# The gradient of an output projection, moved from the attention stage of a fused backward kernel to its last stage

## The chip, the core and the metric

The kernel runs on one NeuronCore of a Trainium2 chip. The core has a matrix engine (TensorE, PE in the profile; its weight loads are shown as PEld), three engines for elementwise work (VectorE or DVE, ScalarE or ACT, GpSimd or POOL), a queue engine (SyncE or SP) that issues most transfers, and 16 DMA engines that carry them. Matrix products land in PSUM, eight banks of 2 KB per partition, and are copied ("evacuated") from there to SBUF by VectorE or ScalarE. The metric is the device time of one execution in microseconds.

## The reference

A gated mix of a sliding-window attention A and a gated feed-forward block B, and the gradients of all its inputs but B_x, which is not used:

```python
q, k, v = qkv[0], qkv[1], qkv[2]                 # 32 heads of 16, from x @ wqkv
scores = jnp.einsum("bhqd,bhkd->bhqk", q, k) * (Dh ** -0.5)
mask = (idx[:, None] - idx[None, :] >= 0) & (idx[:, None] - idx[None, :] < W)   # W = 256
p = _softmax(jnp.where(mask[None, None], scores, -1e9), axis=-1)
o = jnp.einsum("bhqk,bhkd->bhqd", p, v)
a = o.reshape(B, S, D) @ wo
...
h = relu(x @ W_gate) * (x @ W_up);  b = h @ W_down
g = _sigmoid((x * gate_w).sum(-1, keepdims=True))
out = g * a + (1 - g) * b
_grads = _vjp(grad_out)
```

B = 1, S = 2048, D = 512, F = 1376, all in bfloat16. With da = g * grad_out, the gradient of wo (dWo, `out_3`, 512 x 512) is the product of o transposed and da, summed over the 2048 rows.

## The kernel before

Rows are cut into 16 tiles of 128 (t, or q and k for query and key blocks), D into four slices of 128 (c; each holds 8 heads), F into 11 chunks. Three stages follow each other.

**Feed-forward stage.** For every chunk of F and every 512 rows PE makes the gate, the up product and dh; the results h, dgate and dup go transposed to DRAM (`hgu_d`) and PE sums the gradients of W_gate, W_up and W_down. In the same turns `make_da` (L314) scales grad_out by g, and `turn_da` (L319) stores a tile of da in DRAM (`da_d`) and transposes it into SBUF (`da_T`).

**Attention stage.** The loop at L970 runs turns: per slice c 46 of them, each with two pairs of heads. A turn makes scores S and D (L714), the exponential (ScalarE, L747), the mask (GpSimd, L757), the product PP (VectorE, L764), transposes of it by PE (L818) or by DMA (L810), row sums BA (L781, L783) and the products CD (L495, L498) that give dk and dv. `small_ops` (L821) writes dq and o, CD's evacuation dk and dv, into `sts[c]`, 16 tiles by four columns of 128: index 0 to 2 are dq, dk, dv, index 3 is o. It is spilled to `dqkvo_d` in DRAM (L506). PE's remaining time in a turn is filled from a list `bg` of priced pieces: the projections of the next 512 rows (`project_parts`, L137), in c = 0 the rest of the feed-forward gradients (`tail_parts`), and in c = 1, 2, 3 the weight gradients of slice c - 1 (`grad_parts`, L567): first part DC, which is dWo (16 matmuls of 512 columns, L606, with the rows of da loaded back from `da_d`), then four parts of dWqkv (64 matmuls of 384 columns, L603). L990 says how many parts begin in each quarter of a slice: (0, 1, 2, 2). A list `late` holds the loads and transposes of weights for the last stage, popped every second turn (L1070).

**The seam.** After the last turn SP loads what the last stage needs for its first two tiles: `early_group` (L860) the transposed dq, dk, dv and o, `load_group(0)` (L898) the rest, among it duT_g; then the last transposes of W_up into SBUF (L1082), whose last chunk is padded by a GpSimd memset (`clear`, L528), which waits for the transposes. The gradients of slice c = 3 are done here, as `S2["grads"]`: dWqkv for the first 12 tiles within the last turns, then dWo, then dWqkv for the last four tiles. Their stores go over GpSimd's queue (L590).

**Last stage.** Eight groups of two tiles (L1107). For a tile PE makes b in `bps` (11 matmuls of 512 columns, L1117), a in `aps` (4, L1121), and dx in `dxps` (11 + 11 + 12, L1147 and L1173), and adds four columns for the gradient of gate_w (L1157). ScalarE copies and scales `aps` (L1124, L1126), VectorE makes the output `o_sb` (L1128), then VectorE and GpSimd the row sum `dz` (L1132 to L1138), which `dx_sb` (L1179) needs together with `dxps`. `dxps` has two PSUM banks, `bps` and `aps` have one each.

Instructions of an engine are issued in the order in which the code records them; each waits on semaphores for what it reads and for the buffer it writes.

## Time and profile before

| What | Value |
|---|---|
| three runs | 887.89, 894.38, 899.25 us (median 894.38) |
| the profiled execution | 886.93 us, of which the profile's span is 885.2 us |
| feed-forward stage | up to 242 us of the span |
| attention, c = 0, 1, 2, 3 | 105, 114.4, 113.7, 113.5 us (243 to 690 us) |
| seam | 690 to 711 us |
| last stage | 711 to 885 us, a tile 10.7 us |
| DMA | 161.95 MB in 442,156 packets |

A line of the windows gives the length of a stretch, then each engine's busy time and number of instructions, the granted clock of TensorE, the mean busy share of the DMA engines (over 1 where packets overlap in time) and GB/s. A line of the waits names who waited, for whom, the sum in microseconds, how often and the longest. A line of the timeline gives the start, the length, the engine, the line of the code, the operation and its tiles, and in brackets the idle time before it with what ended it. The busy time of one matmul (379 ns for 512 columns) includes its way through the array; matmuls follow each other more closely than that, so their cost is read from a row of many.

### The profile page before, as it was taken

Reading aid. Unit: us, or ns where it says so; the run is one execution under the profiler, and the core shown is the slowest. Engines: PE = TensorE matmul, PEld = TensorE weight load, DVE = VectorE, ACT = ScalarE, POOL = GpSimd, SP = SyncE. Lnnn points to the kernel's source line nnn. Section 1 sums busy time; section 2 is a strip of 40 time slices with the busy share of each in tenths; the row PEclk is TensorE's granted clock in tenths of the full one; section 3 lists DMA queues with packets and bytes.
Section 4 is the critical chain, followed back from the end, with each engine's and each line's share of the span. In section 5 each row is a group of like instructions: output and inputs, shape, how many; then the busy total and the mean of one; then the engine's idle time right before and its main releaser. Section 6 shows DMA issues by size and latency. Waiting matters only on the chain. (4 is left out here: it accounts for less than half of the span.)

```text
span 885.2 us, 29234 instructions
## 1 busy us (share of the span) xinstructions
PE 847.1 (96%) x12415; PEld 557.1 (63%) x12545; DVE 504.3 (57%) x758; ACT 386.2 (44%) x558; POOL 485.0 (55%) x894
## 2 busy tenths in 40 slices
PE   7999999999989999999999999999899999999998
PEld 4556655665557877777777767777677744444443
DVE  4445433333367888877778887787777323232222
ACT  5522222223266676766557655567455311111111
POOL 1645444444357787877668776687676532222221
PEclk9999999999999999999999999999999999999999
DMA  9999999998857999999978999899999999777750
GB/s 278 235 188 218 217 220 223 233 215 194 188 91 119 158 148 160 167 153 172 204 122 146 150 194 189 137 179 159 192 193 182 256 265 269 190 192 191 192 118 25
DMA packets 442156, 161.95 MB, mean 183 GB/s; under 512 B 361640, under 2 KB 439176, under 8 KB 442024
## 3 DMA queue, kind: packets, MB, share of 16 engines
q1 hardware_dynamic: 437896, 152.20, 90.9%
q0 software_dynamic: 2544, 7.34, 2.9%
q8 instruction: 98, 1.61, 0.7%
q10 hardware_dynamic: 1584, 0.53, 0.3%
q14 instruction: 34, 0.28, 0.1%
HBM read 38.44 MB, written 38.34 MB: 87 GB/s over the span
## 5 line engine op out<-in xcount | busy, mean ns | idle before, releaser
L764 DVE TENSOR_TENSOR PP<-PP,D 128x1024 bf16<-128x1024 bf16 (+1 forms) x184 | 219.2, 1191 | 68.2 <-POOL PP L757 24.7
L747 ACT ACTIVATE PP<-S 128x1024 bf16<-128x1024 f32 (+1 forms) x184 | 185.2, 1007 | 100.1 <-PE D L714 49.3
L757 POOL TENSOR_SCALAR_AFFINE_SELECT PP<-PP 128x512 bf16<-128x512 bf16 (+1 forms) x188 | 143.8, 766 | 90.1 <-ACT PP L747 87.4
L74 DVE COPY p<-pt 128x1024 bf16<-128x1024 bf16 x167 | 114.4, 685 | 13.0 <-PE pt L818 12.9
L357 POOL TENSOR_TENSOR hgu<-rg,upm 128x512 bf16<-128x512 bf16 x44 | 50.8, 1155 | 120.5 <-DVE upm L355 103.5
L818 PE MATMUL pt<-ident,PP 128*128 128x128 bf16 x1512 | 114.6, 219 | 0.9 <-issue 0.9
L781 PE MATMUL BA<-KV,PP 128*128 128x33 bf16 x1440 | 106.9, 180 | 3.7 <-ACT BAs L72 2.8
L781 PEld LDWEIGHTS <-PP 128*128 128x128 bf16 x1440 | 85.8, 96 | 31.1 <-issue 12.3
L783 PE MATMUL BA<-KV,PP 128*128 128x17 bf16 x1440 | 102.6, 170 | 0.7 <-issue 0.7
L397 PE MATMUL wps<-hgu_r,x_r 128*128 128x256 bf16 x640 | 96.0, 273 | 0.7
L495 PE MATMUL CD<-rq,p 128*128 128x32 bf16 x1440 | 94.9, 176 | 0.0
L498 PE MATMUL CD<-rq,p 128*128 128x16 bf16 x1440 | 93.6, 169 | 0.0
L783 PEld LDWEIGHTS <-PP 128*128 128x128 bf16 x1440 | 84.8, 96 | 10.7 <-issue 6.4
L818 PEld LDWEIGHTS <-PP 128*128 128x128 bf16 x1512 | 86.3, 97 | 1.2 <-issue 1.2
L714 PE MATMUL S<-zT,K 32*128 32x128 bf16 (+3 forms) x1056 | 77.9, 239 | 5.3 <-ACT PP L747 1.3
L495 PEld LDWEIGHTS <-p 128*128 128x128 bf16 x1440 | 80.7, 95 | 0.3
L498 PEld LDWEIGHTS <-p 128*128 128x128 bf16 x1440 | 80.5, 96 | 0.3
L397 PEld LDWEIGHTS <-x_r 128*128 128x128 bf16 x640 | 62.6, 98 | 28.6
L714 PE MATMUL D<-zT,V 32*128 32x128 bf16 (+3 forms) x1056 | 72.4, 238 | 5.8 <-DVE PP L764 5.2
L355 DVE SCALAR_TENSOR_TENSOR upm<-rg,ups 128x512 bf16<-128x512 bf16 x44 | 30.3, 689 | 79.8 <-PE ups L342 54.8
L1124 ACT COPY a_sb<-aps 128x512 f32<-128x512 f32 x16 | 9.4, 586 | 145.0 <-issue 133.1
L365 POOL TENSOR_TENSOR hgu<-dh_sb,rg 128x512 bf16<-128x512 bf16 x44 | 58.7, 1334 | 9.0 <-ACT dh_sb L363 9.0
(145 smaller groups left out, 1480.6 us busy)
## 6 DMA issues: line engine op xcount, KB each, us to landing
hgu_d<-hgu SPq DMA_DIRECT2D x44, 384.0 KB, 3.3
dqkvo_d<-rows_st SPq DMA_DIRECT2D x14, 512.0 KB, 4.7
dar<-da_d SPq DMA_DIRECT2D x22, 256.0 KB, 5.1
duT_g<-hgu_d SPq DMA_DIRECT2D x8, 640.0 KB, 6.0
dgT_g<-hgu_d SPq DMA_DIRECT2D x7, 640.0 KB
gt<-hgu_d SPq DMA_DIRECT2D x7, 640.0 KB, 5.9
p<-PP SPq DMA_TRANSPOSE x171, 4.2
out_dram<-wst SPq DMA_DIRECT2D x20, 128.0 KB, 3.0
```

The lines of the kernel that those rows point to most:

```text
L74: nc.vector.tensor_copy(out, in_)
L365: nc.gpsimd.tensor_tensor(out=k.hgu[:, 2, :], in0=dh_sb[:], in1=k.rg[:], op=ALU.mult)
L397: nc.tensor.matmul(acc["w"][:, c, :], lhsT=x_r[:, t, c * P:(c + 1) * P], rhs=k.dgu_r[:, :, i, :], start=(go_ and c % 2 == 0), stop=no_, sk ...
L495: nc.tensor.matmul(cd[0][:, h, :], lhsT=p2[:, 0, pr, :], rhs=rq[:, h, 0:2 * Dh], start=cd[1], stop=True, skip_group_check=True)
L498: nc.tensor.matmul(cd[0][:, h, 0:Dh], lhsT=p2[:, 1, pr, :], rhs=rq[:, h, 2 * Dh:3 * Dh], start=False, stop=True, skip_group_check=True)
L714: nc.tensor.matmul(dst, lhsT=proj[(u.c, kb // TPG)][nm + ("", "1")[par]][rows[par], (kb % TPG) * P:(kb % TPG + 1) * P], rhs=proj[(u.c, qb ...
L747: nc.scalar.activation(two[:].rearrange("p x a b q -> p x a (b q)")[:, :, 0, 0:n], flat(us[0].S[:], n), ACT.Exp)
L757: nc.gpsimd.affine_select(out=out, in_=out, compare_op=ALU.is_ge, fill=0.0, base=0 if up else -1, pattern=[[0, 2], [0, b1 - b0], [1 if up ...
L764: nc.vector.tensor_tensor(out=v(1), in0=v(0), in1=flat(vs[0].D[:], n), op=ALU.mult)
L781: nc.tensor.matmul(BA[:, h, 0:33], lhsT=u.PP[:, 0, 2 * i + pr, :], rhs=kv[:, kb % TPG, h, 1:34], start=(first and pr == 0), stop=True, ski ...
L783: nc.tensor.matmul(BA[:, h, 33:50], lhsT=u.PP[:, 1, 2 * i + pr, :], rhs=kv[:, kb % TPG, h, 0:17], start=False, stop=True, skip_group_check ...
L818: nc.tensor.transpose(pt[:, a, b if u.nb == 2 else 2 * u.x + b, :], u.PP[:, a, b, :], ident[:])
```

## The change

1. dWo is no longer a part of `grad_parts`. It is summed in the last stage, in four PSUM banks `wo_ps` that stay open over all 16 tiles. For each tile ScalarE makes `da_b` = grad_out * g; the four matmuls of a tile are issued one tile later, behind the next tile's `aps` (the last tile's at once). At the last tile ScalarE and VectorE evacuate two banks each and SP stores them.
2. `da_d` and all its stores and loads are gone. o comes back row by row from `dqkvo_d` as `o_g`, two transfers a group ahead of grad_out's.
3. The four banks are paid for: `dxps` has one bank instead of two, and the small transpose at the end, `dgw_t`, uses the bank of `aps`.
4. The parts that begin in the quarters of a slice are (0, 2, 1, 1); the extra rules of the credit loop for dWo go. At the seam the last four pieces of dWqkv follow the last turn directly.
5. The SBUF set free gives the tiles P2 14 buffers instead of 12.
6. In slice c = 3, up to query block 12, `late` is popped every fourth turn instead of every second.

The diff, cut to its core:

```diff
-            nc.sync.dma_start(da_d[t * P:(t + 1) * P, :], da_in[t][:])
             nc.sync.dma_start_transpose(out=da_T[t // TPG][:, :, (t % TPG) * P:(t % TPG + 1) * P], in_=da_in[t][:])
...
-                    else:
-                        nc.tensor.matmul(wps, lhsT=sts[c][:, t, 3, :], rhs=rows[t], start=go_, stop=no_)
...
+            if seam:
+                return [lambda p=p, t0=t0: piece(p, t0, t0 == 0, t0 + 4 == NT) for a, b in ((0, NT - 4), (NT - 4, NT))
+                        for p in (0, 2, 1, 3) for t0 in range(a, b, 4)]
+            return [[(0.324, lambda p=p, t0=t0: piece(p, t0, t0 == 0, t0 + step == NT), t0 + step < NT)
+                     for t0 in range(0, NT, step)] for p in range(DC)]
...
-                p2 = pools["p2"].tile([P, 2, 4, P], BF, tag="P2", bufs=12, name="p2")[:]
+                p2 = pools["p2"].tile([P, 2, 4, P], BF, tag="P2", bufs=14, name="p2")[:]
...
-            out = [lambda: nc.sync.dma_start(rest[:, 0:4, :], da_v[:, 0:4, :]),
-                   lambda: nc.sync.dma_start(rest[:, 4:8, :], da_v[:, 4:8, :]), grads]
+            out = [grads]
...
+            o_g = S2["g6"].tile([P, GT, DC, P], BF, tag="o_g", name="o_g")
+            for t in range(GT):
+                t0 = (g * GT + t) * P
+                nc.sync.dma_start(o_g[:, t, :, :], dqkvo_d[t0:t0 + P, :].rearrange("p (c a n) -> p c a n", c=DC, a=4)[:, :, 3, :])
...
-                        for _ in range(((2, 1, 0, 0) if c == 0 else (0, 1, 2, 2))[j // TPG]):
+                        for _ in range(((2, 1, 0, 0) if c == 0 else (0, 2, 1, 1))[j // TPG]):
...
-                if late and (late[0] is not load_wo or turn > NI) and (not us or turn % 2 == 1):
+                if late and (late[0] is not load_wo or turn > NI) and (not us or turn % (4 if us[0].c == DC - 1 and us[0].q < 12 else 2) == 1):
...
+            wo_ps = [ps6.tile([P, D], F32, name=f"wo_ps{c}") for c in range(DC)]
+            pending_wo = []
+
+            def add_dwo(t_, o_, da_):
+                for c in range(DC):
+                    nc.tensor.matmul(wo_ps[c][:], lhsT=o_[:, c, :], rhs=da_[:], start=(t_ == 0), stop=(t_ == NT - 1))
...
+                    da_b = t6.tile([P, D], BF, tag="da_b")
+                    nc.scalar.mul(da_b[:], go_g[:, tl, :], g_all[:, t:t + 1])
+                    pending_wo.append((t, o_g[:, tl, :, :], da_b))
+                    while pending_wo and (pending_wo[0][0] < t or t == NT - 1):
+                        add_dwo(*pending_wo.pop(0))
...
+                    if t == NT - 1:
+                        for c in range(DC):
+                            ws = t6.tile([P, D], BF, tag="wo_s", bufs=DC, name="wo_s")
+                            evac(ws[:], wo_ps[c][:], ("act", "dve")[c % 2])
+                            nc.sync.dma_start(out_3[c * P:(c + 1) * P, :], ws[:])
-                    dxps = ps6.tile([P, D], F32, tag="dxps", bufs=2)
+                    dxps = ps6.tile([P, D], F32, tag="dxps", bufs=1)
...
-                            dgw_t = ps6.tile([P, P], BF, name="dgw_t")
+                            dgw_t = psa.tile([P, P], BF, tag="aps", bufs=1, name="dgw_t")
```

More of the change, by code (lines that the diff above doesn't have):

```diff
@@ L98 @@
     dqkvo_d = dram.tile([S, 4 * D], BF, name="dqkvo_d")
-    da_d = dram.tile([S, D], BF, name="da_d")
     cpool = ctx.enter_context(tc.tile_pool(name="const", bufs=1))
@@ L565 @@
                 15: loads("Wd", B_W_down, 0, "x3") + loads("Wd", B_W_down, 4, "d3") + loads("Wd", B_W_down, 8, "p3") + [load_wo]}
-        def grad_parts(c, rest=None):
-            out = []
-            rows = {}
-            def load_da(i, eng):
-                pool, tag, bufs = (wk, "das", 2) if i in (4, 5) else (gwp, "dar", 4)
-                a = pool.tile([P, 2, D], BF, tag=tag, bufs=bufs, name="dar")
-                for e in range(2):
-                    rows[2 * i + e] = a[:, e, :]
-                eng.dma_start(a[:], da_d[i * 2 * P:(i + 1) * 2 * P, :].rearrange("(t p) d -> p t d", p=P))
-            for i in range(6 if rest is None else 4):
-                load_da(i, nc.sync)
-            if rest is not None:
-                rows.update(rest)
-            hold = {}
-            step = 2 if rest is None else 4
-            def store(part, ws):
-                if part < DC:
-                    to = out_2[part * P:(part + 1) * P, :].rearrange("p (a n) -> p a n", a=3)[:, :, c * P:(c + 1) * P]
-                else:
-                    to = out_3[c * P:(c + 1) * P, :]
-                return lambda: (nc.sync if rest is None else nc.gpsimd).dma_start(to, ws[:])
-            def piece(part, t0, first, last):
-                if first and rest is not None and part < DC:
-                    if "SD"[part // 2] not in hold:
-                        hold["SD"[part // 2]] = ps.tile([P, 2, 4, P], F32, tag="SD"[part // 2], bufs=1, name="wps")
-                    hold[part] = hold["SD"[part // 2]][:, part % 2, 0:3, :]
@@ L597, in piece, with grad_parts @@
+        def grad_parts(c, seam=False):
+            hold = {}
+            step = 4 if seam else 2
+            def piece(part, t0, first, last):
+                if first and seam:
+                    tag = "SD"[part // 2]
+                    if tag not in hold:
+                        hold[tag] = ps.tile([P, 2, 4, P], F32, tag=tag, bufs=1, name="wps")
+                    hold[part] = hold[tag][:, part % 2, 0:3, :]
                 elif first:
-                    hold[part] = ps.tile([P, 3, P] if part < DC else [P, D], F32, tag="tr", bufs=2, name="wps")[:]
+                    hold[part] = ps.tile([P, 3, P], F32, tag="tr", bufs=2, name="wps")[:]
@@ L599, in piece @@
                 wps = hold[part]
                 for t in range(t0, t0 + step):
-                    go_, no_ = first and t == t0, last and t == t0 + step - 1
-                    if part < DC:
-                        nc.tensor.matmul(wps, lhsT=x_r[:, t, part * P:(part + 1) * P], rhs=sts[c][:, t, 0:3, :],
-                                         start=go_, stop=no_)
-                    else:
-                        nc.tensor.matmul(wps, lhsT=sts[c][:, t, 3, :], rhs=rows[t], start=go_, stop=no_)
@@ L607, in piece @@
-                if part == DC and rest is None and t0 + 12 < NT:
-                    ev.setdefault(turn + 1, []).append(("load", lambda: load_da(t0 // 2 + 6, nc.gpsimd)))
+                    nc.tensor.matmul(wps, lhsT=x_r[:, t, part * P:(part + 1) * P], rhs=sts[c][:, t, 0:3, :],
+                                     start=first and t == t0, stop=last and t == t0 + step - 1)
                 if not last:
                     return None
-                if part < DC:
-                    ws = (gwp if rest is None else S2["t6"]).tile([P, 3, P], BF, tag="ws", bufs=2 if rest is None else 5, name="ws")
-                    share(ws[:], wps, 3 * P)
-                    return store(part, ws)
@@ L615, in piece @@
-                ws = (gwp if rest is None else S2["t6"]).tile([P, D], BF, tag="ws", bufs=2 if rest is None else 5, name="ws")
-                share(ws[:], wps, D)
-                return store(part, ws)
-            if rest is None:
-                parts = [(DC, 0, NT)] + [(p, 0, NT) for p in range(DC)]
-            else:
-                for a, b in ((0, NT - 4), (NT - 4, NT)):
-                    if a:
-                        out += [(DC, t0, t0 == 0, t0 + 4 == NT) for t0 in range(0, NT, 4)]
-                    out += [(p, t0, t0 == 0, t0 + 4 == NT) for p in (0, 2, 1, 3) for t0 in range(a, b, 4)]
-                return [lambda a=a: piece(*a) for a in out]
@@ L627, in grad_parts @@
-            for part, a, b in parts:
-                out.append([(0.324 if part < DC else 0.432,
-                             lambda part=part, t0=t0, f=(t0 == a), l=(t0 + step == b): piece(part, t0, f, l), t0 + step < b, part == DC)
-                            for t0 in range(a, b, step)])
-            return out
+                ws = (S2["t6"] if seam else gwp).tile([P, 3, P], BF, tag="ws", bufs=4 if seam else 2, name="ws")
+                share(ws[:], wps, 3 * P)
+                to = out_2[part * P:(part + 1) * P, :].rearrange("p (a n) -> p a n", a=3)[:, :, c * P:(c + 1) * P]
@@ L633, in tail_parts @@
+                return lambda: (nc.gpsimd if seam else nc.sync).dma_start(to, ws[:])
+            if seam:
[3 more added lines that the diff above has]
+                     for t0 in range(0, NT, step)] for p in range(DC)]
         def tail_parts():
@@ L861, in early_group @@
             a = st.tile([P, NT, 4, P], BF, tag="rows_st", name="early")[:].rearrange("p t a n -> p (t a n)")
-            n1 = 4 * DC * GT * P
-            S2["T0"] = a[:, 0:n1].rearrange("p (c s) -> p c s", c=4 * DC)
-            rest = a[:, n1:n1 + 8 * D].rearrange("p (t d) -> p t d", t=8)
-            S2["rows"] = {8 + t: rest[:, t, :] for t in range(8)}
-            da_v = da_d[8 * P:, :].rearrange("(t p) d -> p t d", p=P)
+            S2["T0"] = a[:, 0:4 * DC * GT * P].rearrange("p (c s) -> p c s", c=4 * DC)
             def grads():
-                S2["grads"] = grad_parts(DC - 1, S2["rows"])
-            out = [lambda: nc.sync.dma_start(rest[:, 0:4, :], da_v[:, 0:4, :]),
-                   lambda: nc.sync.dma_start(rest[:, 4:8, :], da_v[:, 4:8, :]), grads]
+                S2["grads"] = grad_parts(DC - 1, True)
+            out = [grads]
             for k in range(4):
@@ L916, in load_group @@
             load_f(duT_g, duT_d, gsl)
+            o_g = S2["g6"].tile([P, GT, DC, P], BF, tag="o_g", name="o_g")
+            for t in range(GT):
+                t0 = (g * GT + t) * P
+                nc.sync.dma_start(o_g[:, t, :, :], dqkvo_d[t0:t0 + P, :].rearrange("p (c a n) -> p c a n", c=DC, a=4)[:, :, 3, :])
             nc.sync.dma_start(go_g[:] if g == 0 else go_g, go_d[gsl, :].rearrange("(t p) d -> p t d", p=P))
-            return hT_g, dgT_g, duT_g, T_g, go_g
+            return hT_g, dgT_g, duT_g, T_g, go_g, o_g
         with tc.manual_schedule():
@@ L936, in background @@
             def background():
-                price, f, more = bg.pop(0)[:3]
+                price, f, more = bg.pop(0)
                 put = f()
@@ L1041 @@
                         for _ in range(2):
-                            if len(S2["grads"]) > 4 + DC:
+                            if len(S2["grads"]) > DC:
                                 S2["grads"].pop(0)()
@@ L1045 @@
                     left = max(1, until - turn)
-                    costs = [(b[0], len(b) > 3 and b[3]) for b in bg]
-                    rest = sum(x for x, dc in costs)
-                    dcs = [x for x, dc in costs if dc]
-                    rate = rest / left
-                    if dcs and len(dcs) < left and not costs[0][1]:
-                        rate = max(rate, (rest - sum(dcs)) / (left - len(dcs)))
+                    rate = sum(b[0] for b in bg) / left
                     credit = min(1.2, credit + rate)
-                    shut = slow = 0
+                    shut = 0
                     while bg and credit >= 0.5 * bg[0][0]:
-                        price, _, more, dc = (bg[0] + (False,))[:4]
+                        price, _, more = bg[0]
                         closes = price > 0 and not more
-                        if dc and slow == (2 if len(dcs) == NT // 2 else 1) or closes and shut == (1 if left > 1 else 2):
+                        if closes and shut == (1 if left > 1 else 2):
                             break
-                        slow += dc
                         shut += closes
@@ L1106 @@
             pending_dgw = None
+            wo_ps = [ps6.tile([P, D], F32, name=f"wo_ps{c}") for c in range(DC)]
[3 more added lines that the diff above has]
+                    nc.tensor.matmul(wo_ps[c][:], lhsT=o_[:, c, :], rhs=da_[:], start=(t_ == 0), stop=(t_ == NT - 1))
             for g in range(NG):
-                hT_g, dgT_g, duT_g, T_g, go_g = grp_next
+                hT_g, dgT_g, duT_g, T_g, go_g, o_g = grp_next
                 if g + 1 < NG:
```

## The prediction

> **What bounds the kernel now.** I read the page's busy table and slices first, then the windows by stage, then who made TensorE wait in attention, and last the timelines around the point where attention hands over to the last stage (below: the seam).

> ```profile
> span 885.2 us, 29234 instructions
> PE 847.1 (96%) x12415; PEld 557.1 (63%) x12545; DVE 504.3 (57%) x758; ACT 386.2 (44%) x558; POOL 485.0 (55%) x894
> PE   7999999999989999999999999999899999999998
> q1 hardware_dynamic: 437896, 152.20, 90.9%
> ...
> 348.00:462.40 114.40, 108.47 (x2496) 81.87 (x2515) 90.87 (x129) 70.76 (x97) 84.76 (x187) 1.00 1.03 163
> 576.30:689.80 113.50, 106.43 (x2490) 81.49 (x2504) 88.25 (x122) 68.80 (x94) 83.50 (x184) 0.98 1.07 183
> 689.90:711.00 21.10, 20.48 (x295) 14.10 (x295) 4.26 (x10) 4.70 (x9) 8.48 (x22) 1.00 1.17 269
> 753.50:881.00 127.50, 126.72 (x626) 58.59 (x638) 37.50 (x83) 14.38 (x26) 27.51 (x36) 1.00 0.63 154
> 140.00:160.00 20.00, 19.89 (x122) 11.89 (x123) 6.29 (x9) 5.30 (x10) 8.97 (x9) 1.00 1.09 221
> ```

> In a window the columns are its length, then the busy time of PE, PEld, DVE, ACT, POOL, then clock, DMA share and GB/s. TensorE (PE) is busy everywhere: 19.89 of 20 us in the feed-forward stage, 95% in an attention pass (c = 1 and c = 3 shown), 99% in the last stage. The DMA engines are as full as PE (share 1.03 to 1.17) up to the seam and have room only in the last stage (0.63). Busy is not the same as limited, so the next question is whether PE work in attention is really paid for. Three windows of twelve turns each, with twelve exponentials (L747) in each, answer it:

> ```profile
> 300.10:325.90 25.80, 12.30 (x12) 1.00 1.05 148
> 373.60:402.90 29.30, 12.30 (x12) 1.00 1.04 143
> 402.90:435.50 32.60, 12.30 (x12) 1.00 1.18 199
> ...
> PE D L714 <- DVE PP L764: 3.8, 11, 0.5
> PE pp L150 <- ACT ws L72: 2.5, 3, 1.2
> PE BA L781 <- ACT BAs L72: 2.1, 8, 0.3
> PE wps L603 <- ACT ws L72: 1.7, 3, 0.6
> ...
> ACT PP L747 <- DMA p<-PP: 3.5, 3, 2.2
> ```

> The first window (c = 0, third quarter) has the projections alone as background; the second (c = 1, second quarter) has 14 dWo matmuls more, the third has 2 dWo and 32 of the dWqkv matmuls more. The turns stretch by 3.5 and 6.8 us. So 14 dWo matmuls cost 0.25 us each. TensorE's named waits over 345 to 692 us are small and none is for a DMA; only ACT waited for transposes, 3.5 us in all.

> The bare price of a matmul, from the chain of waits:

> ```profile
> 705.06 3.18 PE wps L606 x14
> 708.24 1.30 PE wps L603 x8
> 820.74 4.75 PE dxps L1147 x22
> 828.18 2.38 PE bps L1117 x11
> 830.56 0.86 PE aps L1121 x4
> ```

> 4.75 / 22 = 0.216 us for 512 columns; 1.30 / 8 = 0.163 us for 384.

> **Attention.** dWo leaves passes c = 1, 2, 3 (the parts of c - 1), 16 matmuls in each, 48 in all. At the bare 0.216 us that is 10.4 us, at the measured stretch of 0.25 us 12.0 us; I take the middle, 11.2 us off. The dWqkv parts stay 64 matmuls a pass, moved from 0, 32, 32 in the last three quarters to 32, 16, 16: same sum. With dWo go one closing evacuation a pass (inside the 0.25) and the da loads; PE waited for none of them, so they count nothing by themselves. The 3.5 us that ACT waited for transposes could shrink, but the W_gate and W_up transposes now spread into pass c = 3's later turns and take the same queue: 0 taken, -2.2 (ACT's longest such wait) to +2.2 kept. Two more P2 buffers relieve no wait of PE's list: nothing. The 16 da_d stores go from the feed-forward stage, where PE is at 19.89 of 20: nothing.

> **The last stage.** 64 matmuls of 512 columns come in, 4 in each tile 1 to 14 and 8 in the last: 64 x 0.216 = 13.8 us, all on the path, because PE has no gap there. A tile gains on ScalarE the scaling that makes da_b, which runs ahead of the tile's `aps` copies:

> ```profile
> L295 ACT ACTIVATE db_r<-go_in,omg_all 128x512 bf16<-128x512 bf16 x8 | 5.3, 713 | 1.7 <-DVE omg_all L289 1.7
> L72 ACT CAST dst<-dps 128x512 bf16<-128x512 f32 x10 | 5.9, 591 | 0.0
> L74 DVE CAST wst<-wps 128x512 bf16<-128x512 f32 x10 | 6.9, 691 | 16.1 <-ACT wst L72 16.1
> L1179 DVE SCALAR_TENSOR_TENSOR dx_sb<-gw_b,dz,dxps 128x512 bf16<-128x512 bf16 x16 | 12.0, 748 | 33.3 <-PE dxps L1173 33.3
> ```

> 0.71 us a tile on an engine that is busy 14.4 of 127.5 us: nothing. The four evacuations of dWo (two of 0.59 us on ScalarE, two of 0.69 on VectorE) and their stores lie beside the last tile's 34 dxps matmuls, 7.3 us: nothing; if that cover failed, about 1.4 us. The o_g loads, two per group, are 1,024 packets of 256 bytes; 90.9% of 16 engines over 885.2 us and 437,896 packets make 29 ns a packet, so 1,024 x 29 / 16 = 1.9 us of each engine per group of some 23 us, where the share is 0.63: hidden.

> **One bank for dxps.** It had two; now the first dxps matmul of a tile waits until VectorE has read the tile before (`dx_sb`, 0.75 us). Between the two PE runs 11 + 4 + 4 matmuls, 2.38 + 0.86 + 0.86 = 4.1 us, so in the steady state dx_sb is 3.3 us early, and the wait costs nothing. The exception is tile 0, at the seam.

> **The seam.** Its 16 dWo matmuls (of c = 3) go: 16 x 0.216 = 3.45 us less for PE. They were cover for loads that start only when attention's buffers are free:

> ```profile
> early<-da_d SPq DMA_DIRECT2D x2, 512.0 KB, 4.2
> dar<-da_d SPq DMA_DIRECT2D x22, 256.0 KB, 5.1
> ...
> 686.91 2.21 SPq L576 DMA_DIRECT2D dar<-da_d  x4
> 705.80 1.11 SPq L879 DMA_DIRECT2D duT_g<-hgu_d  x1
> 713.94 2.62 SPq L526 DMA_TRANSPOSE d<-in_B_W_up_dram  x2
> 703.30 0.17 PE L498 MATMUL CD<-rq,p 128*128 128x16 bf16 x1
> 720.61 0.81 PE L1147 MATMUL dxps<-d,duT_g 128*128 128x512 bf16 x3
> 724.49 1.03 PE L1147 MATMUL dxps<-x,f 128*128 128x512 bf16 x4
> 719.93 0.52 POOL L529 MEMSET d<- 32x512 bf16 x1 [14.41 <-DMA d<-in_B_W_up_dram]
> 720.40 3.52 POOL L590 DMA_DIRECT2D out_dram<-ws  x5
> 723.92 1.73 POOL L1133 TENSOR_TENSOR amb<-amb,go_g 128x512 f32<-128x512 f32 x1
> 726.69 0.75 DVE L1179 SCALAR_TENSOR_TENSOR dx_sb<-gw_b,dz,dxps 128x512 bf16<-128x512 bf16 x1
> ```

> The last W_up transpose lands and is padded by GpSimd (the memset, done 720.45); the matmul that needs it, the third of the row at 720.61, starts at 721.04. Spare: 0.6 us. With PE 3.45 us earlier it would be 2.9 us late. Behind the memset GpSimd has the ws stores (3.52 us for five; four remain, 2.8), the o_sb store and tile 0's `amb`; then VectorE ends dx_sb of tile 0 at 727.44. In the changed kernel tile 1's dxps waits for that: PE would want it at 724.49 - 3.45 + 0.86 = 721.9, and gets it at 727.44 - 0.7 = 726.7. So if the W_up transposes land as long after attention's end as now, the two waits together cost 4.8 us. They may land sooner: four dar loads (2.21 us of SP's queue, 256 KB each) and the two of early (512 KB each) go, 2 MB, and duT_g, issued 2.3 us after the last CD matmul, can follow it at once; two o_g loads come in ahead of the transposes, 1.9 us of the DMA engines. Ends 0.5 and 5.0 us; as the queue's share there is 1.17 and 2 MB less go through it against 0.25 MB more, I take 2.5.

> PE would stand idle for that time, and the clock can answer:

> ```profile
> 620.00:640.00 20.00, 17.25 (x393) 12.61 (x394) 14.09 (x20) 9.02 (x11) 14.60 (x31) 0.91 1.21 194
> ```

> With 2.75 us idle in 20 the granted clock fell to 0.91 there, 1.8 us lost. [...] I take 0, since the seam now (20.48 of 21.1 busy) kept 1.00, and keep 1.8 for the high end.

> **Sum.** 886.93 (the profiled execution's time) - 11.2 - 3.45 + 13.8 + 2.5 = 888.6, that is +1.7. The profiled execution was quicker than the median of the three runs, 894.38; the four times are 886.93, 887.89, 894.38, 899.25, their middle is 891.1, and 891.1 + 1.7 = 893.

> **Rivals.**
> Slower, by the turns: attention keeps its pace because VectorE sets it (90.9 of 114.4 us busy, and PE did wait 3.8 us for it), so the 11.2 us don't come back while the 13.8 are paid: 893 + 11.2 = 904. It decides when a turn without dWo is no shorter than one with it. Against it: the first window's turns, with no such matmul, are 3.5 us shorter. 7%.

> Slower, by the bank: dx_sb comes late in every tile and PE pays its 0.75 us sixteen times: 893 + 12 = 905. It decides if dx_sb ends over 4.1 us behind a tile's last dxps matmul. The rows put it 3.3 us early; the 33.3 us in its group are VectorE waiting for PE, not the reverse. 5%. [...]

> Slower, by the seam: stall 5.0 and clock 1.8, 893 + 4.3 = 897. 18%.

> Faster, by the queues: with fewer loads ACT's waits for transposes go (-2.2 to -3.5), the seam costs 0.5, attention returns 12.0: 893 - 3 - 2 - 0.8 = 887. For it: shares over 1. Against: PE never waited for a DMA. 15%.

> The forecast itself: 55%, 889 to 896. That the work merely changes place and nothing else is near it.

> **Numbers.** Runs differ by 6 us to either side of their middle; with the forecast, the seam and the queue cases the range is 886 to 901, leaving out the two slow rivals at 904 and half of what the spread adds below. A difference over 2% (17.9 us) is about what a measurement here can tell from no change; no case reaches it alone, only a slow rival with an unlucky run (912) or a chain of gains (877): 0.03 and 0.02, 0.95 within.

> **What would show it.** Attention passes of about 110 us where c = 1 had 114.4 (if 114, the first rival). From the last CD matmul to tile 1's first dxps matmul are 21.2 us now; after it 18.6 if the seam costs nothing, 21.1 by the forecast, with PE's gaps named after GpSimd's memset and VectorE's dx_sb. Tiles of about 11.5 us where 10.7 are now, and no gap ahead of dxps in later tiles; gaps of 0.7 in each are the bank. A total under 880 or over 905 would make the sum wrong.

## The result, and the profile after

| | median of the runs | lowest to highest | profiled execution (its span) |
|---|---|---|---|
| before (6 runs beside the changed kernel) | 895.39 us | 887.89 to 899.25 | 886.93 (885.2) |
| changed (6 runs) | 883.12 us | 882.34 to 884.06 | 882.34 (880.6) |

The ratio is 0.9873 (95% interval 0.9837 to 0.9909): 1.3% less, inside the 2% band and below the range of the prediction. Two things are to be noticed at once. The gain between medians is 12.3 us, between the two profiles 4.6 us; and the runs of before are spread over 11 us, those of the changed kernel over 1.7. The gain was not the same on every chip: the changed kernel but for one small part that proved to cost nothing (e4, e7) was 6.7 and 8.7 us ahead of before on two chips.

The page of the changed kernel, with the busy times and the main DMA queue; the windows behind it are the passes c = 1, 2, 3, the stretch from the last CD matmul to tile 1's first dxps matmul, and the tiles of the last stage:

```profile
span 880.6 us, 29350 instructions
PE 855.1 (97%) x12545; PEld 555.7 (63%) x12545; DVE 507.2 (58%) x763; ACT 395.0 (45%) x569; POOL 478.4 (54%) x887
...
q1 hardware_dynamic: 437144, 145.51, 88.5%
```

```profile
348.00:457.40 109.40, 106.21 (x2501) 80.09 (x2497) 89.98 (x129) 70.25 (x96) 82.41 (x185) 1.00 0.96 149
457.40:566.40 109.00, 106.08 (x2501) 79.99 (x2497) 89.33 (x127) 70.65 (x97) 81.71 (x184) 1.00 0.96 146
566.40:673.00 106.60, 103.90 (x2494) 79.31 (x2489) 88.80 (x125) 68.55 (x92) 82.00 (x183) 1.00 1.08 172
...
686.05:707.00 20.95, 18.93 (x100) 9.03 (x96) 4.37 (x11) 4.90 (x9) 6.66 (x10) 1.00 1.06 240
753.00:880.60 127.60, 124.19 (x619) 56.78 (x617) 35.50 (x78) 19.97 (x36) 24.60 (x32) 1.00 0.59 145
```

The passes were 114.4, 113.8 and 113.6 us, and give back 5.0, 4.8 and 7.0: 16.8 us where 11.2 were forecast. The DMA engines' share fell from 1.03 to 0.96 in c = 1; in c = 3 it stayed over 1 (1.07 before, 1.08 now). The seam answers to what was expected of it; the timeline of the changed kernel (start, length, engine, line, tiles, idle time before with what ended it):

```profile
691.12 4.04 SPq L524 DMA_TRANSPOSE x<-in_B_W_up_dram  x2
695.21 2.60 SPq L524 DMA_TRANSPOSE d<-in_B_W_up_dram  x2
...
686.05 0.17 PE L496 MATMUL CD<-rq,p 128*128 128x16 bf16 x1
700.08 0.52 POOL L527 MEMSET d<- 32x512 bf16 x1 [11.79 <-DMA d<-in_B_W_up_dram]
700.54 2.91 POOL L586 DMA_DIRECT2D out_dram<-ws  x4
703.52 1.67 POOL L1099 TENSOR_TENSOR amb<-amb,go_g 128x512 f32<-128x512 f32 x1
706.22 0.75 DVE L1150 SCALAR_TENSOR_TENSOR dx_sb<-gw_b,dz,dxps 128x512 bf16<-128x512 bf16 x1
707.02 1.02 PE L1118 MATMUL dxps<-x,f 128*128 128x512 bf16 x4 [1.91 <-DVE dx_sb L1150]
```

That is the foretold chain, in its order: memset, four ws stores, `amb`, `dx_sb`, and then PE, idle for 1.91 us. From the last CD matmul it is 707.02 - 686.05 = 21.0 us (forecast 21.1).

The table that the rest leans on is read from the starts of PE's instructions in each trace: the passes c = 1 to 3 together, the drain (from the end of the last turn that makes scores to the last CD matmul), from there to tile 1's first dxps matmul, from that to the end. The time up to pass c = 1 is 347.5 to 348.9 us in all. Each row is one execution.

| Kernel | passes | drain | CD to tile 1 | to the end | span |
|---|---|---|---|---|---|
| before, profile of the prediction | 341.8 | 13.4 | 21.2 | 160.7 | 885.2 |
| e1, before again | 340.2 | 13.2 | 23.4 | 162.0 | 886.8 |
| e9, before, third profile | 341.2 | 15.1 | 23.6 | 161.6 | 889.7 |
| e10, before, fourth profile | 341.4 | 14.0 | 21.7 | 160.7 | 885.9 |
| e5, before, no seam da loads | 342.0 | 13.0 | 21.2 | 161.1 | 885.5 |
| e6, before, no pass da loads | 337.5 | 13.0 | 24.4 | 161.0 | 883.7 |
| e11, before, no da loads by GpSimd | 343.2 | 13.4 | 23.9 | 161.1 | 890.5 |
| e2, before, no da traffic | 337.3 | 13.0 | 21.2 | 161.5 | 881.4 |
| changed | 325.0 | 13.0 | 21.0 | 173.6 | 880.6 |
| e3, changed, da stores and pass da loads back | 328.9 | 13.0 | 21.3 | 174.0 | 884.9 |
| e12, changed, da stores and seam da loads back | 325.1 | 13.3 | 28.7 | 173.7 | 889.2 |
| e8, changed, seam off GpSimd | 325.0 | 13.0 | 19.3 | 173.9 | 878.6 |

### The profile page after: what moved, and what is told of

Read it like the earlier page. It is cut to its first block, busy times and chain, and to the rows that moved or that the text cites. A ratio compares the mean times of both kernels' runs of the same rounds, so it can differ in the third digit from the quotient of the medians.

```text
span 880.6 us, 29350 instructions
## 1 busy us (share of the span) xinstructions
PE 855.1 (97%) x12545; PEld 555.7 (63%) x12545; DVE 507.2 (58%) x763; ACT 395.0 (45%) x569; POOL 478.4 (54%) x887
## 5 line engine op out<-in xcount | busy, mean ns | idle before, releaser
L74 DVE COPY p<-pt 128x1024 bf16<-128x1024 bf16 x164 | 112.3, 685 | 10.9 <-PE pt L779 10.9
L744 PEld LDWEIGHTS <-PP 128*128 128x128 bf16 x1440 | 84.6, 96 | 10.7 <-issue 7.3
## 6 DMA issues: line engine op xcount, KB each, us to landing
dqkvo_d<-rows_st SPq DMA_DIRECT2D x14, 512.0 KB, 3.8
go_in<-in_grad_out_dram SPq DMA_DIRECT2D x4, 512.0 KB, 9.4
```

The costliest lines, as they stand in the source:

```text
L74: nc.vector.tensor_copy(out, in_)
L744: nc.tensor.matmul(BA[:, h, 33:50], lhsT=u.PP[:, 1, 2 * i + pr, :], rhs=kv[:, kb % TPG, h, 0:17], start=False, stop=True, skip_group_check ...
```

## The experiments

The theory ("queue theory" in the first expectations): the move of dWo gives nothing; what gains is that da is no longer stored and loaded. The rival ("work theory"): the move gains, as dWo's matmuls cost more in the turns than in the last stage. The time of before beside each is that of the same chip.

**e1, the kernel before, unchanged.** It tells the chip and the spread apart from the change.

> The kernel before, unchanged, for a second profile. Queue theory (transfers of da make transposes of PP late, ScalarE and then TensorE wait for them, by an amount that differs from run to run): a time of 892 to 899, and a profile in which ScalarE waits for PP transposes for clearly more than the 3.5 us of the first one, in attention. Work theory (only TensorE's own work and the closings of its sums differ; the spread has another origin, the seam or the clock): attention as long as in the first profile, 447.6 us, and the extra time of this run at the seam, in the last stage or in the first stage.

Measured: 891.19 us (888.47 to 897.11), ratio 1.0035 [1.0006, 1.0064], so two groups of runs of one kernel can differ by 0.3% or so. Its profile (888.47, the quickest of its eight runs) lost 2.2 us at the seam that the first profile did not lose. The waits of PE name it:

```profile
PE aps L1121 <- DMA gt<-dqkvo_d: 1.1, 1, 1.1
...
PE dxps L1147 <- DMA x<-in_B_W_up_dram: 0.6, 2, 0.4
...
PE dxps L1147 <- DMA d<-in_B_W_up_dram: 0.3, 1, 0.3
```

The last transposes of W_up (tiles x and d), which had 0.6 us to spare in the prediction's profile, are late here, and so is the transpose that tile 1's `aps` reads. This is not what the queue theory expected: in the passes ScalarE waited 1.9 us for transposes where it had waited 3.5, the passes were 1.6 us shorter, and the excess lay at the seam and behind it (1.3 us from tile 1 on), as the other expectation has it. For the passes this profile decides nothing; for the seam it gives the first hint.

**e2, before without the traffic of da; dWo stays where it was.**

```diff
-            nc.sync.dma_start(da_d[t * P:(t + 1) * P, :], da_in[t][:])
...
-            for i in range(6 if rest is None else 4):
-                load_da(i, nc.sync)
...
+            for t in range(NT):
+                rows[t] = x_r[:, t, :]
...
-            out = [lambda: nc.sync.dma_start(rest[:, 0:4, :], da_v[:, 0:4, :]),
-                   lambda: nc.sync.dma_start(rest[:, 4:8, :], da_v[:, 4:8, :]), grads]
+            out = [grads]
```

> The kernel before without the stores and loads of da: dWo's matmuls stay in attention and at the seam, but read rows of x (so out_3 is not dWo). Queue theory: 884 to 888 and a spread under 3 us, ScalarE's waits for transposes near 0. Work theory: 891 to 896 with a spread of 8 us or more, as before; without the da loads ahead of the seam's loads at most 1 us less.

Measured: 883.15 us (882.32 to 884.87) against 889.68, ratio 0.9932 [0.9907, 0.9957]. This is the changed kernel's time and its small spread, with no dWo moved (dWo's matmuls read rows of x, so their cost stays and `out_3` is not dWo). On the same chip e4, which is the changed kernel but for the spacing of `late`, took 882.94. The windows of the three passes:

```profile
348.50:462.00 113.50, 108.18 (x2497) 81.74 (x2518) 90.71 (x129) 70.77 (x98) 82.96 (x186) 1.00 0.94 145
462.00:575.30 113.30, 107.99 (x2493) 81.66 (x2512) 89.40 (x125) 71.12 (x99) 82.11 (x184) 1.00 0.91 146
575.30:685.80 110.50, 105.54 (x2492) 80.85 (x2508) 88.37 (x122) 69.11 (x94) 82.19 (x182) 1.00 1.04 166
```

From here to the changed kernel the passes fall by 12.3 us (337.3 to 325.0), 12.3 / 48 = 0.256 us for each dWo matmul, and the last stage gains 12.1: the move is worth -0.8 us of span, no more than the profiles of one kernel differ. The rival falls.

**e3, the changed kernel with the stores and the passes' loads put back** (nothing reads them).

```diff
+            nc.sync.dma_start(da_d[t * P:(t + 1) * P, :], da_in[t][:])
...
+            if not seam:
+                for i in range(6):
+                    load_da(i, nc.sync)
+                for i in (6, 7):
+                    ev.setdefault(turn + 5 + i, []).append(("load", lambda i=i: load_da(i, nc.gpsimd)))
...
-                p2 = pools["p2"].tile([P, 2, 4, P], BF, tag="P2", bufs=14, name="p2")[:]
+                p2 = pools["p2"].tile([P, 2, 4, P], BF, tag="P2", bufs=12, name="p2")[:]
```

> The changed kernel with the 16 stores of da and the eight loads in each of three passes put back (the loaded rows are not used), P2 again with 12 buffers. Queue theory: 887 to 894 with a spread of several us, late transposes back. Work theory: 883 to 885, spread under 3 us.

Measured: 885.16 us (883.56 to 888.11), 2.0 above the changed kernel's median and 2.2 above e4, its neighbour on the chip. That is under the 887 to 894 of the theory and just over the 883 to 885 of the rival: the traffic costs here, but less than was expected. In the profile, one of the longer runs (886.63), the passes are 3.9 us longer, 2.7 of it in c = 3, the rest within 0.4. ScalarE now waits for the transposes of PP; the changed kernel has no such row:

```profile
ACT PP L721 <- DMA p<-PP: 7.0, 7, 1.6
```

**e4 and e7, two small parts of the change undone:** late transposes every second turn, and 12 P2 buffers.

```diff
-                if late and (late[0] is not load_wo or turn > NI) and (not us or turn % (4 if us[0].c == DC - 1 and us[0].q < 12 else 2) == 1):
+                if late and (late[0] is not load_wo or turn > NI) and (not us or turn % 2 == 1):
```

> The changed kernel with the W_gate and W_up transposes popped every second turn in the last pass as before. If the spacing matters: 1 to 4 us slower and a wait of ScalarE for a PP transpose around the start of pass c = 3. If it does not: within 0.7 us of 883.1.

> The changed kernel with 12 P2 buffers instead of 14 and nothing else. If the buffers matter, part of the 2.0 us of the kernel with the da traffic put back is theirs: 884 to 885. If the traffic alone made them: 882.7 to 883.6.

Measured: 882.94 us (882.65 to 883.53) and 882.88 (881.12 to 884.7). Both lie within 0.3 us of the changed kernel's median, so neither part has a price that shows here.

**e5 and e6, the traffic in halves:** before without the seam's loads of da, and before without the passes' loads.

```diff
-            for i in range(6 if rest is None else 4):
+            for i in range(6 if rest is None else 0):
...
-            out = [lambda: nc.sync.dma_start(rest[:, 0:4, :], da_v[:, 0:4, :]),
-                   lambda: nc.sync.dma_start(rest[:, 4:8, :], da_v[:, 4:8, :]), grads]
+            out = [grads]
```

```diff
-            for i in range(6 if rest is None else 4):
+            for i in range(0 if rest is None else 4):
...
-                if part == DC and rest is None and t0 + 12 < NT:
-                    ev.setdefault(turn + 1, []).append(("load", lambda: load_da(t0 // 2 + 6, nc.gpsimd)))
```

> The kernel before without the six da loads at the seam alone (dWo of c = 3 reads rows of x, so that quarter of out_3 is not dWo); stores and the loads of the three passes stay. Seam theory (the loads of the seam have 0.6 us to spare in the first profile, and 2 MB of da ahead of them push the W_up and T transposes past that in most runs): 885 to 887.5, spread 4 us or less. Attention theory (the 24 loads in the passes are the cost): 888 to 890, spread as before.

> The kernel before without the 24 da loads of the passes alone (dWo of c = 0, 1, 2 reads rows of x, so those quarters of out_3 are not dWo); stores and the seam's loads stay. Seam theory: 885.5 to 888, about 3 us off from attention, spread still several us. Attention theory: 882.5 to 884.5, spread under 3 us.

Measured, against 891.61: 887.41 us (885.16 to 893.13), ratio 0.9949 [0.9914, 0.9985], and 886.31 us (882.32 to 891.09), ratio 0.9933 [0.9901, 0.9965]. The totals alone leave it open: e5 has the time that the seam theory gave and the spread that the attention theory gave, e6 the time of the seam theory. The profiles, one of each, part the traffic by place: e5 keeps the long passes (342.0) and has the undisturbed seam (21.2), e6 has the short passes (337.5) and a seam that is 3.2 us late. Each keeps a spread of 8 to 9 us (in e5 by two runs of ten); in e2, without both and without the stores, it is 2.6 us.

**e8, the changed kernel with the seam's chain taken off GpSimd:** the four stores go over ScalarE's queue and ScalarE pads W_up's last chunk.

```diff
-                return lambda: (nc.gpsimd if seam else nc.sync).dma_start(to, ws[:])
+                return lambda: (nc.scalar if seam else nc.sync).dma_start(to, ws[:])
...
-            clear("Wu")
...
+                    if t == 0:
+                        pad = W6[("Wu", FC - 1)][0:FC * P - F, :]
+                        nc.scalar.mul(pad, pad, 0.0)
```

> The changed kernel with the four dWqkv stores of the seam issued by ScalarE and the last W_up chunk padded by ScalarE behind tile 0's copies, so that GpSimd multiplies tile 0's row product without waiting for the W_up transposes. If GpSimd's queue is what holds dx_sb of tile 0 and with it the one dxps bank: no wait of dxps for dx_sb at tile 1, 1.5 to 2.2 us faster than 883.1, that is 881 to 881.6. If the bank's wait has another cause or the W_up transposes then bind instead: 882.5 to 883.5.

Measured: 881.53 us (880.36 to 885.63), ratio to before 0.9871 [0.9827, 0.9914]: 1.6 us under the changed kernel's median, as expected, though the runs overlap and were taken at another time. The timeline of PE at tile 1 has no idle time left ahead of dxps:

```profile
700.47 0.38 PE L1120 MATMUL dxps<-d,duT_g 128*128 128x512 bf16 x1 [0.19 <-ACT d L1094]
...
703.92 1.03 PE L1065 MATMUL wo_ps<-da_b,o_g 128*128 128x512 bf16 x4
704.79 1.03 PE L1120 MATMUL dxps<-x,f 128*128 128x512 bf16 x4
```

So the 1.6 us between 20.97 and 19.33 were what GpSimd's queue cost, as the prediction's step on the seam has it. This kernel has the lowest median of the study.

**e9 and e10, the kernel before twice more,** for the profile of a longer run.

> The kernel before, unchanged, for a third profile. Theory (the traffic of da costs through transposes that land late): what this execution takes over the 886.93 us of the first profile lies in two places only, the passes c = 1 to 3 (114.4, 113.8, 113.6 us there; their floor by the kernel without the traffic is 113.5, 113.3, 110.5) and the stretch from the last CD matmul to tile 1's first dxps (21.2 us; 23.4 in the second profile), with waits for DMA named at both. Rival (the spread has nothing to do with the traffic): a slower execution is longer in the feed-forward stage (242.3 us) or in the tiles of the last stage (10.7 us) too.

> As the third look: by the theory an execution of 892 us or more has its excess in the passes c = 1 to 3 and in the stretch between the last CD matmul and the third tile of the last stage, and both the feed-forward stage (242.3 us) and the later tiles (10.7 us) are as in the first profile, within 0.5 us and 0.2 us; by the rival they are not.

Measured: 891.4 and 887.63 us, one run each; neither reached the 892 us that the second expectation speaks of. Against e2, e9 is 8.3 us longer: passes 3.9, drain 2.1, seam 2.4, all else -0.1. The feed-forward stage is 242.4 us and the time from tile 1 on 161.6 (e2: 242.5 and 161.5), so for this execution the rival, a spread without place, falls. The traces give three mechanisms, all in e9. First, GpSimd issues two of the loads in each pass, and a mask stands behind them (timeline of GpSimd, VectorE, PE):

```profile
393.74 1.64 POOL L576 DMA_DIRECT2D dar<-da_d  x2
395.39 0.65 POOL L757 TENSOR_SCALAR_AFFINE_SELECT PP<-PP 128x512 bf16<-128x512 bf16 x1
...
396.07 1.22 DVE L764 TENSOR_TENSOR PP<-PP,D 128x1024 bf16<-128x1024 bf16 x1 [0.99 <-POOL PP L757]
...
397.35 0.23 PE L714 MATMUL D<-zT,V 16*128 16x128 bf16 x2 [0.47 <-DVE PP L764]
```

That turn (number 21 of the pass, from 0) takes 2.84, 2.67 and 2.79 us in the three passes, 2.18 in e2: 1.8 us, and it is so to 0.02 us in all four profiles of before. (e3 issues its two GpSimd loads in other turns, one at a time, and doesn't rebuild this stall.) Second, at the seam the loads stand on SP's queue ahead of everything that the last stage needs (timeline of SP, e9, then e2):

```profile
686.66 2.22 SPq L576 DMA_DIRECT2D dar<-da_d  x4
688.93 7.88 SPq L874 DMA_TRANSPOSE early<-dqkvo_d  x2
...
715.09 3.88 SPq L526 DMA_TRANSPOSE x<-in_B_W_up_dram  x2
719.01 3.26 SPq L526 DMA_TRANSPOSE d<-in_B_W_up_dram  x2
```

```profile
681.70 6.00 SPq L867 DMA_TRANSPOSE early<-dqkvo_d  x4
...
700.56 5.84 SPq L525 DMA_TRANSPOSE x<-in_B_W_up_dram  x2
```

Two transposes take 7.88 us of the queue behind the loads, four take 6.00 without them. The first W_up transposes are issued 10.6 us after the last CD matmul in e9, 1.8 in e2 (5.1 in the prediction's profile, 10.4 in e1, 8.2 in e10); GpSimd's memset starts 19.6, 12.3, 16.6, 19.3 and 17.7 us after it. By the 0.6 us to spare in the prediction's profile, PE can take 16.6 + 0.6 = 17.2. Third, two stops of PE with nothing named but issue (0.96 and 1.11 us), in the last section.

**e11, before without GpSimd's six loads of da;** and **e12, the changed kernel with the da stores and the seam's loads put back** (and 12 P2 buffers).

```diff
+            else:
+                rows.update({t: x_r[:, t, :] for t in range(12, NT)})
...
-                if part == DC and rest is None and t0 + 12 < NT:
-                    ev.setdefault(turn + 1, []).append(("load", lambda: load_da(t0 // 2 + 6, nc.gpsimd)))
```

> The kernel before without the two da loads that GpSimd issues in each of the passes c = 1 to 3 (six in all); for the last four tiles dWo's matmuls of the passes read rows of x instead, so dWo is wrong and its cost the same. Theory: GpSimd's 1.64 us of issuing (L576) stands ahead of a mask, VectorE waits 0.99 us for that mask, PE 0.47 for VectorE, and the turn is 0.5 to 0.7 us longer, once a pass. So the second quarter of each pass becomes 0.4 to 0.7 us shorter than in the profiles of before (c = 1: 28.7 where it was 29.4 to 29.8), 1.3 to 2 us over the three passes, and the 21st turn 2.2 us where it was 2.7 to 2.8. Rival (it is the bytes that cost, whoever issues them): six loads less of 28 change a pass by under 0.2 us and the 21st turn stays at 2.7.

Measured: the turn is 2.18, 2.18 and 2.19 us, so the mechanism holds; but the gain is not in the total, 892.23 us in one run. In c = 1 and 2 the second quarter is 0.6 and 0.5 us shorter than in the quickest of the four profiles of before, but the first quarter is 26.5 and 26.3 us, 1.0 longer than in the prediction's profile. In c = 3 the second quarter is 30.7 us where it was 29.2, a transpose of PP lands so late there that ScalarE waits 3.6 us (timeline of ScalarE), and the granted clock over 620 to 640 us is 0.86:

```profile
632.62 1.02 ACT L747 ACTIVATE PP<-S 128x1024 bf16<-128x1024 f32 x1 [3.63 <-DMA p<-PP]
```

In this one run, what the removed loads gave back was lost elsewhere to the rest of the traffic; one run can't say whether that is the rule.

```diff
+            nc.sync.dma_start(da_d[t * P:(t + 1) * P, :], da_in[t][:])
...
+            if seam:
+                for i in range(4):
+                    load_da(i, nc.sync)
...
+            out = [lambda: nc.sync.dma_start(rest[:, 0:4, :], da_v[:, 0:4, :]),
+                   lambda: nc.sync.dma_start(rest[:, 4:8, :], da_v[:, 4:8, :]), grads]
```

> The changed kernel with the da stores and the seam's da loads put back (four of 256 KB and two of 512 KB, ahead of the transposes of dq, dk, dv, o on SP's queue; nothing reads them, the result is the same) and P2 back at 12 buffers, which e7 showed to be worth nothing. Theory: the loads stand ahead of the last W_up transposes on the queue, so these are issued 8 to 11 us after the last CD matmul (5.1 now), GpSimd's memset starts 17 to 20 us after it (14.0 now), dx_sb of tile 0 is late by as much, and tile 1's dxps begins 24 to 27 us after the last CD matmul (21.0 now); now and then a block of PE's instructions comes late before the last CD matmul, too (0 to 2.5 us). Median 886 to 889. Rival (the seam's loads cost only where dWo is computed there, as in the kernel before): memset at 14 to 15 us, tile 1's dxps at 21 to 21.5, median 883 to 884.

Measured: 889.92 us (888.64 to 890.88), above the 886 to 889 of the theory. The W_up transposes are issued 12.4 us after the last CD matmul, the memset starts at 21.7, tile 1's dxps at 28.7. The waits of PE at the seam; the one for dx_sb is in the changed kernel, too (1.91 us), the others are new:

```profile
PE bps L1092 <- DMA f<-hgu_d: 3.4, 1, 3.4
...
PE dxps L1132 <- DVE dx_sb L1164: 1.9, 1, 1.9
...
PE dxps L1132 <- DMA d<-in_B_W_up_dram: 1.2, 1, 1.2
PE dxps L1132 <- POOL d L529: 1.2, 1, 1.2
```

2 MB of loads that nobody reads (the stores, which end with the feed-forward stage, left the time up to pass c = 1 at 348.4 us, the changed kernel at 348.1) cost 6.8 us between the medians (883.12 was taken at another time) and 7.7 us of the way to tile 1's dxps. The new waits are 5.8 us of the 7.7; most of the remaining 1.9 is the 1.7 us that the matmuls right after the stop of 3.4 us took beyond their price (see the last section). The ten runs lie within 2.2 us: here the loads cost time and make little spread. In the kernel before, dWo's 16 matmuls stood there as cover, 3.45 us; without them PE is at tile 0's bps before its f has landed, too.

## Why the prediction missed

**Right, by mechanism and nearly by size.** The last stage: +13.8 us, of which tile 0's four matmuls (0.86) lie ahead of tile 1's dxps and 12.9 behind it; the profiles say 173.6 - 160.7 = 12.9 (12.1 against e2). The seam: a stall of 2.5 us by the chain memset, ws, amb, dx_sb; it was 1.91, and e8 removed it by moving that chain alone. That the whole way to tile 1 came to 21.0 for 21.1 is partly luck: the stall was 0.6 us shorter, and what lies beside it 0.5 longer than forecast. The clock kept 1.00 over that stop of 1.91 us, as was assumed. One dxps bank in the later tiles, the evacuations, the o_g loads, the two P2 buffers, the spacing of `late` at nothing: no wait of PE for dx_sb but that one, and e4 and e7 within 0.3 us. The da stores at nothing: the feed-forward stage is 242.3, 242.5 and 242.5 us in before, e2 and the changed kernel.

**Right, but mis-sized.** Attention without dWo's matmuls: 11.2 forecast, 12.3 measured between e2 and the changed kernel, past the upper bound of 12.0 by 0.3. The nearness is in part luck. The 0.25 us for a matmul came from twelve turns that held turn 21 with its GpSimd loads; in e2 the same twelve turns take 28.71 us, and (28.71 - 25.77) / 14 is 0.21, the bare price. The rest of the 12.3, about 1.2 us a pass, goes with the last two matmuls, the closing of the sum and the moved dWqkv parts; no run takes these apart.

**Wrong: "the da loads; PE waited for none of them, so they count nothing by themselves".** The rows were read as written, and the conclusion did not follow. Against e2 (337.3) the passes are 2.9 to 4.5 us longer in the four profiles of before, and e3's are 3.9 longer than the changed kernel's, through three engines' queues: in the kernel before 1.8 of it is GpSimd's issuing ahead of a mask, which PE's list shows as a wait for VectorE; some is ScalarE waiting for transposes (it waited 3.5, 1.9, 4.0 and 2.7 us for those of PP in the four); some is PE standing with nothing named but issue (1.0 to 2.8 us). None of these says DMA in PE's list of waits. Turn by turn against e2, the 4.5 us of the prediction's profile are in the main 1.8 in turn 21 of the three passes, 0.8 in turn 10 of c = 3, where PE stands 0.66 with nothing named but issue, and 2.0 in its turns 24 and 25, where the clock was 0.50 for 3.42 us after a transpose that ScalarE waited 2.18 for. The step asked who waits for a load, and not what stands behind its issue on the engine and the queue that it goes through.

**Wrong: the base of the sum.** The sum against the profiled execution was 888.6, and it came out as 882.3: 5.6 us of the 6.3 are the passes (4.5 of loads, 1.1 of the matmuls' price). Another 4.2 us were added by "891.1 + 1.7 = 893", which takes the spread of before for something that any kernel on this chip has. The spread was part of what the change removes. One source of it is the 0.6 us that W_up had to spare in the prediction's profile, the quickest of the four; it is used up in the three others (23.4, 23.6 and 21.7 us where it was 21.2). It is not the only one, as e5 keeps 8 us of spread with the seam's loads gone. e2, with no da traffic, runs within 882.32 and 884.87; before, beside it, took 885.03 to 894.68. The granted clocks of the single runs say what the longest ones have in common. Of the 23 runs of before beside e5 to e8, the four at 1.00 took 887.8 to 890.4 us, the four at 0.989 to 0.992 took 896.3 to 899.8. A mean clock lower by 0.009 over 886 us is 8 us of PE's time at full speed, about what parts the two groups (8.5 us between their medians). So the greater part of the spread comes with a lower clock; the changed kernel's runs are at 0.998 to 1.00.

**The rivals.** By the turns and by the bank are refuted by passes of 109.4 and by the single wait for dx_sb; by the seam, by a stall of 1.91 at full clock. By the queues, given 15%, comes nearest: fewer loads do shorten attention. Its 887 stands on the 893; the same corrections on the sum of 888.6 give 888.6 - 5.8 = 882.8, where 882.34 was profiled. That this fits is partly luck, since the loads gave 4.5 where it has 3, and the seam did not come down to 0.5. Its reason, ScalarE's waits for transposes, is only one of the ways found.

What stays open: how the passes' loss beyond turn 21 splits between late transposes, the stops that end in issue and the clock from run to run; and what set off the lower clock in the runs of before at 896 us and more, as none of them was profiled.

## What to carry to other kernels

A transfer that nobody waits for had a price here (the loads of e3, which nothing reads, made the passes 3.9 us longer): find what stands behind it on its issuing engine and its queue, and count that. If runs of a kernel spread by 1%, do not take one execution as its base: compare the granted clocks of the runs, profile more than one of them, and look for a transfer with under 1 us to spare (here W_up, 0.6). Here, moving matmuls from one full stage to another was worth next to nothing (-0.8 us of span); what they carried along (loads, banks, queues) decided.

## What the runs showed of the hardware

**PE stopped where the profile names nothing but issue.** In e9's drain PE stops twice in the midst of a row of like matmuls (timeline of PE; then its row for one of the two queues that the profile calls instruction):

```profile
693.10 0.28 PE L818 MATMUL pt<-ident,PP 128*128 128x128 bf16 x2 [0.96 <-issue]
...
702.33 0.18 PE L498 MATMUL CD<-rq,p 128*128 128x16 bf16 x1 [1.11 <-issue]
```

```profile
q8 instruction: 98, 1.61, 0.8%
```

**The clock halved where PE was thinly fed, and not at one longer stop.** PE's stop of 1.91 us at the changed kernel's seam kept 1.00. In e12 a stop of 3.36 us, for tile 0's f, was followed by slow matmuls: from 693.16 us on, eight of 384 columns and three of 512 took 3.63 us where their price of 0.163 and 0.216 makes 1.95. The 1.7 us more are 3.4 us at half speed, an estimate. In the prediction's profile PE worked 1.59 of 3 us behind ScalarE's late transpose, with no single stop over 1.2 us, and the clock dropped right after (windows of before; the clock is the third number from the end):

```profile
632.00:635.00 3.00, 1.59 (x32) 1.02 (x28) 2.36 (x4) 1.86 (x3) 1.70 (x5) 1.00 0.90 235
635.00:640.00 5.00, 4.51 (x69) 2.90 (x69) 1.91 (x2) 1.66 (x3) 2.54 (x7) 0.66 1.20 193
```

The clock was 0.50 there from 635.18 to 638.60 us, 3.42 us. PE's stops just before, 0.32 and 1.17 us, were shorter than the one that cost nothing at the seam. So the length of one stop does not decide here; what does is not shown.
